# One core, decode attention over a 64k cache: heads in turn through one ring of 4 MB loads, in place of all keys first and all values after

## Chip, cores, metric

One core of one Trainium2 chip. The metric is the device time of one execution in microseconds (us). Times are medians of runs in the fast state, each measured beside runs of the kernel before on the same chip. A ratio is the mean time of one kernel's fast runs over that of the other's fast runs of the same rounds, so it is not quite the ratio of the medians that stand beside it.

## The reference, cut to what matters

```python
# x: 1 x 1 x 448; k_cache, v_cache: 1 x 8 heads x 65536 keys x 256, bf16
q = (layernorm(x) @ wq)                      # 16 query heads, two to each key head
scores = q . k * 256 ** -0.5                 # per head, over 65536 keys
o = softmax(scores) @ v
out = x + o @ wo + moe_branch(layernorm(x))  # the second branch has 4.8 MB of weights
```

Everything is bf16. The two caches are 537 of the 549 MB that are read, and each value is read once and used for two query heads.

## The kernel before

It works in two stages. The first reads the keys of all eight heads, four heads at a time. TensorE transposes each block of 128 keys by 128 positions, VectorE and ScalarE copy the result from PSUM (where this kernel has TensorE's results), TensorE multiplies by the query (QK) and joins the four heads' scores (JT in the code). Then one softmax is made for all heads. The second stage reads all values and multiplies them by the probabilities (P.V). Loads are 2 MB each, in six buffers, of which two lie over the query weights.

```python
JN_K = 16; HPC = 2; JV = 32; KV_NBUF = 6; NTB = 6; PV_COLGROUPS = 1
# ... loads, issued by SyncE in the order of use: all keys, then all values
for cc in range(total):
    buf = cc % KV_NBUF
    if cc >= KV_NBUF:
        wait("sp", "pe", ("KFREE", cc - KV_NBUF))
    # ... keys: 2 heads x 16 keys per partition; values: 32 keys per partition
    sp.dma_start(kvK[buf], src).then_inc(semK[buf], 16)
# ... transposes: 8 of 128 x 128 into one PSUM bank
for hf in range(NH):
    for jj in range(GNV):
        ins = pe.matmul(ps_t[tb][:, blk * P:(blk + 1) * P],
                        lhsT=kvK[buf][:, mm, nn0 + jj, hf * P:(hf + 1) * P],
                        rhs=ident_bf[:, :], is_transpose=True, start=True, stop=True)
# ... QK: four column groups of the array, one head in each
ins = pe.matmul(qb[po:po + rep, 0:512], lhsT=qT_sb[:, hf, h * rep:(h + 1) * rep],
                rhs=kt_buf[kt][:, hf * 512:(hf + 1) * 512],
                start=(hf == 0), stop=(hf == NH - 1), tile_position=(0, po))
# ... P.V: one accumulation for a head, two keys per matmul
ins = pe.matmul(ob[0:2 * rep, 0:2 * Dh], lhsT=lhsT, rhs=kvV[buf][:, j:j + 2, :],
                start=(n == 0), stop=(n + 2 >= NPP))
# ... the order on TensorE
for s in range(NSET):            # all keys
    # ... transposes of set s + 1, JT of set s - 1, QK of set s
pe_phase2a()                     # maximum over all scores, then the exponentials on ScalarE
for v in range(NCHV):            # all values
    pe_PV_chunk(v)
```

## Time and profile before

| | kernel before |
|---|---|
| time, median (range) | 1345.17 us (1344.43 to 1345.67) |
| profiled span | 1344.0 us |
| TensorE busy, granted clock | 85%, 0.986 |
| bytes moved, mean rate | 550.94 MB, 410 GB/s |
| rate with keys (200 to 700 us) | 407 GB/s |
| rate with values (740 to 1320 us) | 428 GB/s |

The prediction shows the lines behind this table. Two more are needed later. The first is from the page's table of DMA queues (packets, MB, share of the sixteen engines' span). The second is from the windows view (window; busy times of the engines; granted clock, DMA share, GB/s).

```profile
q8 instruction: 107, 1.75, 0.5%
1330.00:1336.00 6.00, 3.65 (x17) 1.31 (x18) 0.00 (x0) 0.00 (x0) 0.00 (x0) 1.00 0.35 147
```

The page labels queue 8 as instruction: it carries the program of an engine, in 107 pieces of 16 KB, the first at 27.5 us and the last at 1333.9 us, so while the kernel runs. It looks negligible. In the last six microseconds of loads the rate is 147 GB/s and the DMA share 0.35: the sixteen DMA engines do not finish together (the landings of the last load lie between 1330.9 and 1335.9 us).

### The profile page before, as it was taken

Reading aid. Unit: us, or ns where it says so; the run is one execution under the profiler, and the core shown is the slowest. Engines: PE = TensorE matmul, PEld = TensorE weight load, DVE = VectorE, ACT = ScalarE, POOL = GpSimd, SP = SyncE. Lnnn points to the kernel's source line nnn. Section 1 sums busy time; section 2 is a strip of 40 time slices with the busy share of each in tenths; the row PEclk is TensorE's granted clock in tenths of the full one; section 3 lists DMA queues with packets and bytes.
Section 4 is the critical chain, followed back from the end, with each engine's and each line's share of the span. In section 5 each row is a group of like instructions: output and inputs, shape, how many; then the busy total and the mean of one; then the engine's idle time right before and its main releaser. Section 6 shows DMA issues by size and latency. Waiting matters only on the chain.

```text
span 1344.0 us, 29602 instructions
## 1 busy us (share of the span) xinstructions
PE 1146.2 (85%) x13639; PEld 720.9 (54%) x13639; DVE 550.0 (41%) x859; ACT 429.6 (32%) x554; POOL 3.1 (0%) x19
## 2 busy tenths in 40 slices
PE   4979989999999999999996998777767777777776
PEld 4857867787777877777773443222222222222222
DVE  2767767777877878787773000000000000000000
ACT  1544645565555555555557600000000000000000
POOL 0000000000000000000000000000000000000000
PEclk9999999999999999999997899999999999999999
DMA  9999999999999999999997999999999999999996
GB/s 369 420 383 420 420 400 420 417 414 403 405 410 407 407 398 407 397 406 409 402 407 325 430 428 427 428 428 427 428 426 428 428 429 428 428 428 428 428 428 277
DMA packets 60738, 550.94 MB, mean 410 GB/s; under 512 B 4227, under 2 KB 10118, under 8 KB 11014
## 3 DMA queue, kind: packets, MB, share of 16 engines
q1 hardware_dynamic: 60610, 549.05, 98.5%
q8 instruction: 107, 1.75, 0.5%
q14 instruction: 17, 0.14, 0.0%
q10 hardware_dynamic: 4, 0.00, 0.0%
HBM read 549.03 MB, written 0.00 MB: 409 GB/s over the span
## 4 chain that ended last, share of the span: by engine, by line
PE 55%; DMA 40%; DVE 4%; ACT 1%; issue 0%; SPq 0%; DVEq 0%; ACTq 0%
DMA kv_buf<-in_A_v_cache_dram 34%; PE ps_t L359 33%; PE ps_t L513 10%; PE ps_q L384 9%; DMA kv_buf<-in_A_k_cache_dram 3%; DMA regA<-in_A_k_cache_dram 2%; DVE kt_buf L619 2%; PE ps_s L403 1%; DVE m1p L645 1%; PE ps_q L437 1%; DVE S_sb L641 1%; PE ps_t L453 1%; ACT S_sb L844 0%; ACT kt_buf L621 0%; PE ps_t L466 0%
## 5 line engine op out<-in xcount | busy, mean ns | idle before, releaser
L619 DVE COPY kt_buf<-ps_t 128x1024 bf16<-128x1024 bf16 x768 | 505.6, 688 | 170.6 <-PE ps_t L359 94.7
L513 PE MATMUL ps_t<-kv_buf,S_sb 128*4 128x512 bf16 x1376 | 313.4, 382 | 92.7 <-DMA kv_buf<-in_A_v_cache_dram 87.5
L359 PEld LDWEIGHTS ps_t<-ident_bf,kv_buf 128*128 128x128 bf16 x5504 | 313.2, 99 | 106.9 <-DVE kt_buf L619 70.2
L359 PE MATMUL ps_t<-ident_bf,kv_buf 128*128 128x128 bf16 x5504 | 341.8, 221 | 32.2 <-DMA kv_buf<-in_A_k_cache_dram 17.3
L621 ACT ACTIVATE kt_buf<-ps_t 128x1024 bf16<-128x1024 bf16 x256 | 262.0, 1023 | 299.5 <-PE ps_q L384 298.7
L513 PEld LDWEIGHTS ps_t<-kv_buf,S_sb 128*4 128x4 bf16 x1376 | 111.6, 85 | 290.6 <-DMA kv_buf<-in_A_v_cache_dram 121.6
L762 DVE CAST ob_sb<-ps_t 128x512 bf16<-128x512 f32 x8 | 5.5, 692 | 451.9 <-PE ps_t L513 451.9
L513 PE MATMUL ps_t<-regA,S_sb 128*4 128x512 bf16 x672 | 153.7, 383 | 43.1 <-DMA regA<-in_A_v_cache_dram 43.1
L359 PEld LDWEIGHTS ps_t<-ident_bf,regA 128*128 128x128 bf16 x2688 | 151.8, 98 | 48.8 <-DVE kt_buf L619 34.4
L359 PE MATMUL ps_t<-ident_bf,regA 128*128 128x128 bf16 x2688 | 165.7, 220 | 12.0 <-DVE kt_buf L619 7.4
L384 PE MATMUL ps_q<-kt_buf,qT_sb 128*2 128x512 bf16 x2048 | 154.9, 379 | 0.0
L513 PEld LDWEIGHTS ps_t<-regA,S_sb 128*4 128x4 bf16 x672 | 54.7, 85 | 139.8 <-DMA regA<-in_A_v_cache_dram 59.4
L629 ACT ACTIVATE s_1<-ps_q 98x512 bf16<-98x512 f32 x128 | 75.6, 591 | 0.9 <-PE ps_q L384 0.9
L629 ACT ACTIVATE s_0<-ps_q 98x512 bf16<-98x512 f32 x128 | 75.6, 591 | 0.0
L770 DVE TENSOR_TENSOR oT_sb<-ps_q,rs 128x4 bf16<-128x4 f32 x8 | 1.3, 162 | 95.3 <-PE ps_q L533 95.3
L844 ACT ACTIVATE S_sb<-S_sb,negmax 128x512 bf16<-128x512 bf16 x16 | 36.8, 2744 | 3.0 <-DVE negmax L715 3.0
L403 PE MATMUL ps_s<-sel_bf,s_0 128*128 128x8 bf16 x512 | 31.4, 167 | 1.7 <-ACT s_0 L629 1.7
L403 PE MATMUL ps_s<-sel_bf,s_1 128*128 128x8 bf16 x512 | 31.4, 167 | 0.8 <-ACT s_1 L629 0.7
L384 PEld LDWEIGHTS ps_q<-kt_buf,qT_sb 128*2 128x2 bf16 x2048 | 26.2, 79 | 5.7
L403 PEld LDWEIGHTS ps_s<-sel_bf,s_0 128*128 128x128 bf16 x512 | 26.4, 97 | 2.2 <-ACT s_0 L629 2.2
L403 PEld LDWEIGHTS ps_s<-sel_bf,s_1 128*128 128x128 bf16 x512 | 26.1, 97 | 1.7 <-ACT s_1 L629 1.7
L729 DVE TENSOR_TENSOR gs_sb<-ps_t,sg_sb 128x14 f32<-128x14 f32 x1 | 0.2, 173 | 45.0 <-ACT sg_sb L854 45.0
(70 smaller groups left out, 110.1 us busy)
## 6 DMA issues: line engine op xcount, KB each, us to landing
kv_buf<-in_A_k_cache_dram SPq DMA_DIRECT2D x86, 2048.0 KB, 14.4
kv_buf<-in_A_v_cache_dram SPq DMA_DIRECT2D x86, 2048.0 KB, 25.7
regA<-in_A_k_cache_dram SPq DMA_DIRECT2D x42, 2048.0 KB, 14.0
regA<-in_A_v_cache_dram SPq DMA_DIRECT2D x42, 2048.0 KB, 25.7
wo_sb<-in_A_wo_dram SPq DMA_DIRECT2D x1, 3584.0 KB, 21.8
regA<-in_A_wq_dram SPq DMA_DIRECT2D x1, 3072.0 KB, 10.3
regF<-in_B_w_down_dram SPq DMA_DIRECT2D x1, 1568.0 KB, 22.0
regF<-in_B_w_gate_dram SPq DMA_DIRECT2D x1, 1344.0 KB, 13.1
```

The source lines that it names most:

```text
L359: ins = pe.matmul(ps_t[tb][:, blk * P:(blk + 1) * P], lhsT=kvK[buf][:, mm, nn0 + jj, hf * P:(hf + 1) * P], rhs=ident_bf[:, :], is_transpos ...
L384: ins = pe.matmul(qb[po:po + rep, 0:512], lhsT=qT_sb[:, hf, h * rep:(h + 1) * rep], rhs=kt_buf[kt][:, hf * 512:(hf + 1) * 512], start=(hf ...
L403: ins = pe.matmul(ps_s[:, col:col + QW], lhsT=s2[s % 2][:, jj * P:(jj + 1) * P], rhs=sel_bf[:, :], start=True, stop=True)
L437: ins = pe.matmul(ps_p0[0:P, col:col + 1], lhsT=wq_sb[0:r, kc, q * Dh + hf * P:q * Dh + (hf + 1) * P], rhs=xnT_sb[0:r, kc:kc + 1], start=( ...
L453: ins = pe.matmul(ps_f[0:P, base + f:base + f + 1], lhsT=wsb[0:r, kc, f * P:(f + 1) * P], rhs=xnT_sb[0:r, kc:kc + 1], start=(kc == 0), sto ...
L513: ins = pe.matmul(ob[0:2 * rep, 0:2 * Dh], lhsT=lhsT, rhs=kvV[buf][:, j:j + 2, :], start=(n == 0), stop=(n + 2 >= NPP))
L619: ins = eng.tensor_copy(out=kt_buf[kt][:, :], in_=ps_t[tb][:, :])
L621: ins = eng.activation(out=kt_buf[kt][:, :], in_=ps_t[tb][:, :], func=ACTF.Copy)
L629: ins = act.activation(out=s2[s % 2][0:QROWS, :], in_=ps_q[0:QROWS, :], func=ACTF.Copy) if ctx.emit else None
L641: ins = dve.tensor_copy(out=S_sb[:, quad, n_lo:n_lo + SB_N, :], in_=ps_s[:, 0:W])
L645: ins = dve.tensor_reduce(out=m1p[:, quad, k, :], in_=S_sb[:, quad, n_lo:n_lo + SB_N, :].rearrange("p n q -> p q n"), axis=AX.X, op=ALU.max)
L844: ins = act.activation(out=ap, in_=ap, func=ACTF.Exp, bias=negmax[:, c:c + 1], scale=1.0, accum_out=rowsum[:, c:c + 1])
```

## The change

The intent is to keep the DMA engines at their rate from the start to the end. Heads are worked through one by one. Each head has its own softmax, and the key chunks of head h+1 alternate with the value chunks of head h. All loads, weights too, go through one ring in SBUF of 168 KB per partition, 4 MB a load (32 KB per partition). P.V accumulates in four column groups of the array, which are added when the result is transposed. The core of the diff, cut:

```diff
-JN_K = 16
-HPC = 2
-JV = 32
-KV_NBUF = 6
+RING = 86016                      # bf16 elements per partition: 5.25 loads of 64 x 256
+K_CHUNKS = [64] * 8
+V_LAST = [64] * 7 + [32, 16, 8, 8]
-PV_COLGROUPS = 1
 ...
+    for n, k_ in enumerate(ks):
+        kv_item(*k_)
+        if n >= len(K_FIRST) + 1:
+            v_next()              # one value chunk after each key chunk
+    while vs:
+        v_next()
 ...
+    def prog_sp():
+        for n, it in enumerate(items):
+            for m in range(max(0, it["need"] - 8), it["need"] + 1):
+                wait("sp", "pe", ("FREE", m))      # the loads whose space this one takes
 ...
-                ins = pe.matmul(ob[0:2 * rep, 0:2 * Dh],
-                                lhsT=lhsT, rhs=kvV[buf][:, j:j + 2, :],
-                                start=(n == 0), stop=(n + 2 >= NPP))
+                ins = nc.tensor.matmul(ps_o[32 * g:32 * g + 2 * rep, :], lhsT=S[:, k:k + 2, :].rearrange("p n i -> p (n i)"), rhs=kv[:, j:j + 2, :],
+                                       start=(k < 2 * NG), stop=(k >= NPP - 2 * NG), tile_position=(0, 32 * g))
 ...
+            post("dve", lambda: dve_scopy(h, k))
+            if k == NSB - 1:
+                post("dve", lambda: dve_m1(h))
+                defer(2, lambda: pe_m1t(h), ("sm", h))   # the head's softmax, some sets later
```

## The prediction

> **What bounds the kernel now.** I read the forty slices first, because the shares of section 1 (PE 85%, DVE 41%) average over two stages with different limits. Page of the kernel before, sections 2 and 3:
>
> ```profile
> PE   4979989999999999999996998777767777777776
> DVE  2767767777877878787773000000000000000000
> DMA  9999999999999999999997999999999999999996
> GB/s 369 420 383 420 420 400 420 417 414 403 405 410 407 407 398 407 397 406 409 402 407 325 430 428 427 428 428 427 428 426 428 428 429 428 428 428 428 428 428 277
> q1 hardware_dynamic: 60610, 549.05, 98.5%
> ```
>
> One slice is 33.6 us. Slices 0 to 20 are the keys, 22 to 39 the values. The values run flat at 428 GB/s, the keys at about 405, with a hole (325) between. The DMA digit is 9 in both stages, so it does not tell a full queue from one that is merely never empty; the GB/s row does.
>
> What sets the rate in each stage, from the windows (columns: window, PE, PEld, DVE, ACT, POOL busy, granted clock, DMA share, GB/s) and the list of waits (who waited for whom: total us, times, longest):
>
> ```profile
> 200.00:700.00 500.00, 482.08 (x8429) 394.15 (x8426) 398.87 (x611) 289.51 (x384) 0.00 (x0) 1.00 1.00 407
> 740.00:1320.00 580.00, 454.45 (x2116) 167.93 (x2113) 7.50 (x20) 19.65 (x18) 0.00 (x0) 0.99 1.01 428
> SPq L299 <- PE ps_t L359: 562.1, 64, 20.1
> PEld ps_t L359 <- DMA kv_buf<-in_A_k_cache_dram: 17.9, 2, 9.0
> PE ps_t L513 <- DMA kv_buf<-in_A_v_cache_dram: 87.5, 71, 2.8
> ```
>
> In the key stage PE is busy 482 of 500 us and waits for a key load only twice; the load queue waits for PE's transposes instead (562 us). The chain of waits shows the pace there: sets of 1.05 MB start every 2.51 us (1.89 transposes, 0.08 join, 0.53 QK), and every 16 sets one is 4.0 us because the score copy (0.69) and the maximum (1.1) sit ahead of VectorE's PSUM copies. That is 16 x 2.51 + 1.5 = 41.7 us for 16.8 MB, 402 GB/s: PE with its evacuation is the bound. In the value stage PE waits for every chunk: DMA is the bound. The seam and the end, in the chain:
>
> ```profile
> 721.40 4.84 ACT S_sb L844 x4
> 726.34 33.32 PE ps_t L513 x144
> 1310.29 25.63 DMA kv_buf<-in_A_v_cache_dram
> 1335.97 3.63 PE ps_t L513 x16
> ```
>
> The softmax over all heads stands between the stages with all buffers full of values: the windows 725 to 730 and 730 to 735 moved 52 and 134 GB/s.
>
> [...] QK, which already uses four column groups:
>
> ```profile
> L384 PE MATMUL ps_q<-kt_buf,qT_sb 128*2 128x512 bf16 x2048 | 154.9, 379 | 0.0
> L513 PE MATMUL ps_t<-kv_buf,S_sb 128*4 128x512 bf16 x1376 | 313.4, 382 | 92.7 <-DMA kv_buf<-in_A_v_cache_dram 87.5
> ```
>
> The same 512 columns cost 154.9/2048 = 76 ns each there, against 313.4/1376 = 228 ns in P.V. [...] after 8.4 us of waiting at 92 us the window 100 to 105 has clock 0.50 and 32 transposes took 3.60 us, not 1.96.
>
> **The change, part by part.** All four parts serve one aim: never let DMA fall below its rate.
>
> 1. Interleaving. After head 0, key and value chunks of 4.19 MB alternate. A pair takes 8.39 MB / 428 = 19.6 us of DMA. PE per pair: keys 4 sets, 10.05 us, plus a quarter of the 1.5 us stall, 10.4; values 32 matmuls x 76 ns = 2.4. Together 12.9 us warm. PE will then idle some 6.7 us per pair and fall to half clock; from the cold example a first set costs about 4.6 instead of 2.5, so I add 2.6: 15.5 us, still 4 below DMA. PE leaves the path. Gain: the key stage from 110 to 700 us ran at 408 instead of 428, 590 x (1 - 408/428) = 27.6 us, of which about 1 us stays for the output weights; plus about 1 us before 110.
>
> 2. Softmax per head. Head h's maximum and two exponentials (2 x 2.74 us) run while the loads of other heads stream. Gain: the seam, 5 x (1 - 52/428) + 5 x (1 - 134/428) = 7.8 us. Its new cost, some 10 us of stall in a PE that has 4 to 6.7 us of slack per pair, is absorbed by the ring.
>
> 3. Ring. From the sizes in the code, 13 to 17 MB of later loads lie between most loads and the one whose space they take (10 to 13 MB around the FFN weights and each output-weight piece): 23 to 40 us of DMA. PE's lag must stay below that. Its worst is head 0, keys alone: PE at 10.4 us per 4.19 MB against 9.8 of DMA, starting about 10 us late because of the 128 query matmuls (9.06 us). After 40 sets, ten chunks' worth, the lag is 10 + 10 x 0.6 = 16 us, below 39. I expect no blocking.
>
> 4. P.V in four groups: 467 us of PE busy (313.4 + 153.7) become about 155. Hidden as such, but part 1 would fail without it: 32 x 228 ns = 7.3 us of values plus 10.4 + 2.6 is 20.3, above 19.6. The last chunk shrinks from 16 matmuls (3.63 us) to 4: 3.2 us off the end.
>
> What stays: the start and small rows of weights (slices 0 to 3 lose about 9 us, of which I keep 8), the end after the values (ob copy to output 4.4 us) and the skew of the engines before it (from 1330 to 1335 the rate falls 295, 213, 180, 164, 33).
>
> Sum from above: 26.6 + 1 + 7.8 + 3.2 = 38.6 off 1345, 1306. Sum from below: all transfers, 550.94 MB / 428 = 1287; start and small rows 8.6; skew 3.8; last matmuls, rest and the gap between span and time 0.4 + 4.4 + 1.0. Total 1305. Loads grow from 8 or 16 KB to 32 KB per partition: key windows with a full queue (424 to 430 for 8 KB) hardly differ from value windows (428 for 16 KB), so I allow 0.2%, 3 us, and predict **1303 us**.
>
> **Rivals.** (a) **PE stays the bound.** For: its clock will drop, and ScalarE's exponentials block its share of the PSUM copies 5.5 us per head, with one PSUM buffer per position now (four, not six). Against: 4 us of slack per pair even cold, and a PE that falls behind is busy and warm. If the pair took 22 us, 55 pairs would add 130 us: slower than before. I give this 3%. (b) **The ring blocks** in head 0 or at the FFN weights, where only 10 MB (23 us) are ahead: a few stalls of 5 to 10 us, 1310 to 1325. For: lag 16 us there at its worst plus ffn1's 112 matmuls (7.6 us before). Against: by then five pairs have won back 4 us each. 10%. (c) **The rate of 32 KB rows.** Nothing in this trace has rows as long. At 432 GB/s the time falls to about 1293; if two alternating streams cost 1% it is 1316. (d) **The time is hidden anyway**: that the keys at 405 are DMA's own limit with 8 KB rows, and stay. Against: windows of 428 with key loads while PE waits (95 to 100 us), and PE waiting for keys only twice.
>
> **Range and chances.** The floor of 428 and the ends are measured; what spreads is the rate (plus or minus 0.7%, 9 us) and small ring stalls. Range 1292 to 1314. 2% faster means below about 1318.5: 0.91. Within 2%: 0.07, from (b) or (c) at their bad ends. Slower: 0.02, from (a).
>
> **What would show it.** Right: GB/s about 428 in nearly all slices from the third on, no hole; the chain mostly of DMA; PE waiting for the ring's loads in every pair; P.V matmuls at some 75 to 80 ns of busy time each; PE share about 65 to 70% with granted clock clearly below 1, at no cost; the queue's waits for PE long in total but never emptying DMA. Wrong: slices around 400 with PE at 9 (rival a), single low slices near 100 or 200 us (b), or a flat rate other than 428 (c).

## The result, and the profile after

The changed kernel takes **1310.41 us** (1310.06 to 1310.87, 4 runs) against 1345.17. The ratio is 0.9738, with a 95% interval of 0.9724 to 0.9752: faster by 2.6%. That is inside the stated range, 7 us above the stated time.

Page of the changed kernel, slices (32.7 us each) and queues:

```profile
PE   5998765867866767667767668667677577676444
PEclk9999878878879888788788788788788887888666
DMA  9999999999999999999999999999999999999995
GB/s 383 426 427 429 415 382 432 430 430 431 431 430 425 432 428 430 431 428 431 430 430 427 429 429 430 430 430 430 428 428 429 428 426 433 429 429 416 434 426 213
q1 hardware_dynamic: 24578, 549.04, 98.4%
q8 instruction: 107, 1.75, 0.5%
```

The rate is flat from slice 6 to slice 38 (mean 429.1), and the hole between the stages is gone. TensorE falls to some 7 tenths, and its granted clock to 8. Apart from the start (slice 0, 383), the low slices are 4 and 5 (415, 382), with the small rows of the second branch's weights (a row of 896 bytes took 41 ns, 21.9 bytes per ns, one of 3584 bytes 151 ns, 23.7; a row of 32 KB took 1215 ns, 27.0), 36 (416, a loss of 1 us), and the last with 213.

Windows of the changed kernel (columns as before), in the steady part and at the end of the loads:

```profile
250.00:1280.00 1030.00, 714.31 (x10482) 541.22 (x10479) 409.55 (x669) 324.18 (x421) 0.00 (x0) 0.83 1.00 429
1288.00:1303.40 15.40, 7.15 (x64) 1.58 (x64) 0.00 (x0) 0.00 (x0) 0.00 (x0) 0.57 0.42 177
```

For 1030 us the engines move 429 GB/s; then for 15 us they are 42% busy. Before, this ragged end had 6 us. From the list of waits of the changed kernel (total us, times, longest), TensorE's wait for keys and the load queue's wait for TensorE:

```profile
PE ps_t L370 <- DMA ring<-in_A_k_cache_dram: 308.0, 55, 10.4
SPq L298 <- PE ps_s L431: 870.1, 61, 19.6
```

TensorE now waits for nearly every key chunk. The queue waits for TensorE too, 870 us in all, but its loads are issued some 40 us before they land (44.3 us for keys, 37.9 for values), so DMA does not run dry. The groups (count, then busy us and mean ns):

```profile
L370 PE MATMUL ps_t<-ident_bf,ring 128*128 128x128 bf16 x8192 | 598.1, 241 | 309.8 <-DMA ring<-in_A_k_cache_dram 308.0
L658 PE MATMUL ps_o<-ring,S_sb 128*4 128x512 bf16 x2048 | 136.6, 412 | 48.1 <-DMA ring<-in_A_v_cache_dram 46.1
L398 PE MATMUL ps_q<-kt_buf,qT_sb 128*2 128x512 bf16 x2048 | 167.9, 407 | 0.0
```

P.V fell from 467 us of busy time to 136.6. Over 2048 matmuls that is 67 ns each: the 412 ns of the line are the time of one from start to end, and several overlap. The last instructions, in order of time (start, duration):

```profile
1303.33 0.60 PE L658 MATMUL ps_o<-ring,S_sb 128*4 128x512 bf16 x4 [0.64 <-DMA ring<-in_A_v_cache_dram]
1303.98 0.69 DVE L511 CAST ob_sb<-ps_o 100x512 bf16<-100x512 f32 x1 [61.95 <-PE ps_o L658]
1304.73 0.27 PE L531 MATMUL ps_m<-sel_bf,ob_sb 100*128 100x2 bf16 x4 [0.80 <-DVE ob_sb L511]
1305.24 1.65 PE L557 MATMUL ps_m<-ring,oT_sb 128*1 128x448 bf16 x4 [0.25 <-DVE oT_sb L518]
1306.93 0.61 DVE L543 TENSOR_TENSOR res_bf<-ps_m,rowsf 1x448 bf16<-1x448 f32 x1 [1.74 <-PE ps_m L557]
```

From the last landing to the end of the span it is 5.8 us. From 1303.4 to 1309 us the granted clock is 0.50, and the output product takes 1.65 us.

**Where the predicted sum and the result part.** From the slices: 550.89 MB at 429.1 GB/s are 1284 us; slices 0 to 5 lose 8.5 us against that rate; slice 39 loses 16.5. Together 1309, the span. The prediction had 1284 (1287 less 3 for longer rows), 8.6, and for the end 3.8 + 0.4 + 4.4 = 8.6, and 1 us between span and time. So one term was wrong: the end. Of the 16.5 us, 5.8 follow the last landing. The other 10.7 are the ragged end, which the prediction calls skew and put at 3.8.

**A first look at the ragged end.** The trace records sixteen landings for each load, and for 97% of the span fifteen to seventeen data packets are in flight; each landing is read here as that of one of the sixteen DMA engines. Sorted, for loads along the changed kernel's run (us; this table is worked out from those records):

```
load complete   1st engine    8th      9th     16th    pieces of program so far
      83.2         81.4       82.3     82.9     83.2        8
     247.2        243.0      243.9    246.6    247.2       24
     447.0        439.7      441.4    446.3    447.0       ~40
     647.0        635.1      637.8    644.8    647.0       ~57
     845.6        830.5      834.2    843.3    845.6       ~73
    1044.1       1025.9     1030.5   1041.8   1044.1       ~90
    1303.3       1285.2     1287.7   1301.0   1303.3      107
```

The sixteen engines part into two groups of eight. At the end the first group has finished about 1286 us, the other about 1302. The distance between the groups' means, set against the number of pieces fetched on queue 8, is a straight line through zero: 1.31 us for each piece per engine of a group of eight, correlation 0.994. Against time the line is as straight (0.993), so this alone does not tell pieces from bytes. Single pieces do show in the records: between the loads complete at 547.2 and 606.7 us five pieces were fetched, and five landings of the late group moved back against the early group, each by about 1.4 us, while its other three stayed. The packet of a piece itself took 1.07 us (median), a data row of the same 16 KB 0.62. In the kernel before the same 107 pieces give no such line (correlation 0.08): the groups were 3.9 us apart at 282 us but only 1.3 at 650 us, after 80 pieces, and in its value stage, with 17 pieces, the distance grew from 0.5 to 3.4.

This suggests **theory F**: each 16 KB piece of TensorE's program that is fetched holds one of eight DMA engines back by 1.31 us. While TensorE sets the pace the late engines catch up; when DMA sets it they fall behind for good, and the late group ends the kernel. Its **rival R** is that eight engines are slower by nature, so that the distance grows with bytes.

### The profile page after: what moved, and what is told of

It reads as the page before. It is cut to its first block, busy times and chain, and to the rows that moved or that the text cites.

```text
span 1309.1 us, 29128 instructions
## 1 busy us (share of the span) xinstructions
PE 921.8 (70%) x13690; PEld 701.4 (54%) x13690; DVE 537.7 (41%) x885; ACT 426.6 (33%) x555; POOL 4.5 (0%) x34
## 2 busy tenths in 40 slices
DMA packets 24701, 550.89 MB, mean 421 GB/s; under 512 B 2371, under 2 KB 6214, under 8 KB 7366
## 3 DMA queue, kind: packets, MB, share of 16 engines
q8 instruction: 107, 1.75, 0.5%
## 4 chain that ended last, share of the span: by engine, by line
DMA 75%; PE 25%; SPq 0%; issue 0%; DVE 0%
DMA ring<-in_A_k_cache_dram 68%; PE ps_t L370 17%; DMA ring<-in_A_v_cache_dram 7%; PE ps_q L398 4%; PE ps_o L658 2%; PE ps_s L431 1%; PE ps_m L557 0%; SPq L298 0%; PE ps_m L608 0%; PE ps_m L531 0%; DVE ob_sb L511 0%; DVE res_bf L543 0%; PE ps_m L502 0%; DVE oT_sb L518 0%
## 5 line engine op out<-in xcount | busy, mean ns | idle before, releaser
L370 PE MATMUL ps_t<-ident_bf,ring 128*128 128x128 bf16 x8192 | 598.1, 241 | 309.8 <-DMA ring<-in_A_k_cache_dram 308.0
L370 PEld LDWEIGHTS ps_t<-ident_bf,ring 128*128 128x128 bf16 x8192 | 552.0, 110 | 423.8 <-DMA ring<-in_A_k_cache_dram 336.1
L352 DVE COPY kt_buf<-ps_t 128x1024 bf16<-128x1024 bf16 x768 | 493.2, 686 | 636.9 <-PE ps_t L370 636.2
L383 ACT ACTIVATE s<-ps_q 98x512 bf16<-98x512 f32 x256 | 152.9, 597 | 335.5 <-PE ps_q L398 335.5
L658 PE MATMUL ps_o<-ring,S_sb 128*4 128x512 bf16 x2048 | 136.6, 412 | 48.1 <-DMA ring<-in_A_v_cache_dram 46.1
L398 PE MATMUL ps_q<-kt_buf,qT_sb 128*2 128x512 bf16 x2048 | 167.9, 407 | 0.0
L658 PEld LDWEIGHTS ps_o<-ring,S_sb 128*4 128x4 bf16 x2048 | 49.3, 89 | 122.1 <-DMA ring<-in_A_v_cache_dram 54.3
L431 PE MATMUL ps_s<-sel_bf,s 128*128 128x8 bf16 x1024 | 64.9, 169 | 0.7 <-ACT s L383 0.7
L431 PEld LDWEIGHTS ps_s<-sel_bf,s 128*128 128x128 bf16 x1024 | 57.2, 102 | 2.4 <-ACT s L383 1.6
L477 ACT ACTIVATE S_sb<-S_sb,negmax 128x512 bf16<-128x512 bf16 x16 | 13.4, 861 | 7.3 <-DVE negmax L470 7.2
## 6 DMA issues: line engine op xcount, KB each, us to landing
ring<-in_A_k_cache_dram SPq DMA_DIRECT2D x63, 4096.0 KB, 44.3
ring<-in_A_v_cache_dram SPq DMA_DIRECT2D x63, 4096.0 KB, 37.9
ring<-in_A_wo_dram SPq DMA_DIRECT2D x8, 448.0 KB, 30.3
ring<-in_A_wq_dram SPq DMA_DIRECT2D x1, 3072.0 KB, 10.4
ring<-in_A_k_cache_dram SPq DMA_DIRECT2D x2, 1024.0 KB, 15.1
```

Of the source, the lines that this page charges most:

```text
L352: op(e, ("EV", g), lambda x: x.tensor_copy(out=kt[:, :], in_=tb[:, :]))
L370: ins = nc.tensor.matmul(ps_t[g % NTB][:, blk * P:(blk + 1) * P], lhsT=kv[:, j + GN * m + jj, hf * P:(hf + 1) * P], rhs=ident_bf[:, :], is ...
L383: op("act", ("EVQ", s), lambda e: e.activation(out=s2[s % 2][0:QROWS, :], in_=ps_q[0:QROWS, :], func=ACTF.Copy))
L398: ins = nc.tensor.matmul(ps_q[32 * m:32 * m + rep, 0:512], lhsT=qT_sb[:, hf, h * rep:(h + 1) * rep], rhs=kt[:, hf * 512:(hf + 1) * 512], s ...
L431: ins = nc.tensor.matmul(o, lhsT=s2[s % 2][:, jj * P:(jj + 1) * P], rhs=sel_bf[:, :, :], start=True, stop=True)
L477: op("act", ("EXPI", h, i), lambda e, i=i: e.activation(out=S[:, :, i], in_=S[:, :, i], func=ACTF.Exp, bias=negmax[:, h, i:i + 1], scale=1 ...
```

## The experiments

All eleven ran without an error. Each is given with its median, its ratio to the kernel before in the same rounds, and the difference to the changed kernel's ratio (0.9738) times 1345 us, because the kernel before differed by up to 2 us between batches. A ratio's interval is about plus or minus 0.0014, or 2 us. The changed kernel was not run again in these batches, so a difference of two ratios is uncertain by about 2.7 us (an estimate from the two intervals).

| run | median us | ratio | against the changed kernel |
|---|---|---|---|
| a_halfT: half of the transposes | 1304.97 | 0.9690 | -6.5 us |
| a_vsplit: P.V matmuls in two | 1314.09 | 0.9758 | +2.7 us |
| a_poolfetch: longer idle program | 1332.09 | 0.9891 | +20.6 us |
| a_low8: one load on few engines | 1341.46 | 0.9963 | +30.3 us |
| a_pv1: P.V in one group | 1312.82 | 0.9747 | +1.2 us |
| a_seq: no interleaving | 1311.23 | 0.9737 | -0.1 us |
| a_ring3: ring of 3.25 loads | 1327.01 | 0.9856 | +15.9 us |
| b_pv4: kernel before, P.V in four | 1340.70 | 0.9957 | -5.8 us to before |
| a_wolow8: output weights on few engines | 1338.05 | 0.9944 | +27.7 us |
| a_wolow8half: every other head so | 1325.50 | 0.9850 | +15.1 us |
| a_f32T: transposes of 4-byte pairs | 1305.51 | 0.9699 | -5.2 us |

### Fewer instructions, the same loads: a_halfT

```diff
-        for hf in range(NH):
+        for hf in range(1):
             for jj in range(GN):
                 blk = hf * GN + jj
```

The PSUM banks are zeroed once, so that nothing unwritten is read. The scores lack half their positions; the output still passed the comparison, presumably because the scores here are so small that the softmax is nearly uniform.

> The changed kernel with the second half of all key transposes left out (4096 matmuls and 4096 weight loads fewer; wrong result on purpose; the instruction memory of TensorE shrinks from 107 to 75 pieces of 16 KB). Theory F: each piece of program that is fetched holds back one of eight DMA engines by 1.31 us, and these eight set the end. Then 32 pieces fewer bring the last landing 32/8 x 1.31 = 5.2 us forward: about 1305 us, and the gap between the two groups of eight engines at the end falls from 16.2 to about 11 us. Rival R (eight engines are slower by nature, so the gap grows with bytes): 1310 us and a gap of 16 us, because TensorE is off the path either way.

Measured: 1304.97 us. The queue table of this run:

```profile
q8 instruction: 75, 1.23, 0.4%
```

The pieces fell from 107 to 75. That is 32 pieces for the 8192 TensorE instructions left out, 256 instructions a piece, so queue 8 carries TensorE's program. The late group ended at 1296.0 us instead of 1301.8, 5.8 earlier (expected 5.2). The distance at the end is 13.2 us, not 11: the early group too came in earlier, by 2.9 us, which F does not say; the two groups seem tied to some degree. Rival R, which allowed no change, falls: no byte of data was taken away. That TensorE became faster is no explanation by itself, for it is off the path (a_pv1 below slows it a good deal for 1.2 us).

### More instructions, the same work: a_vsplit

```diff
-                ins = nc.tensor.matmul(ps_o[32 * g:32 * g + 2 * rep, :], ..., rhs=kv[:, j:j + 2, :], ...)
+                for n2 in range(2):
+                    ins = nc.tensor.matmul(ps_o[32 * g:32 * g + 2 * rep, n2 * Dh:(n2 + 1) * Dh], ..., rhs=kv[:, j + n2, :], ...)
```

> The changed kernel with every P.V matmul of 512 columns split into two of 256 (right result, the same columns; 2048 matmuls and 2048 weight loads more, 16 pieces of program more). Theory F: 16/8 x 1.31 = 2.6 us later, 1313 us, gap 18.8 us. Rival R: 1310 us, gap 16 us.

Measured: 1314.09 us, +2.7 us by the ratios. The queue table of this run:

```profile
q8 instruction: 123, 2.02, 0.6%
```

There are 123 pieces. The late group ended 3.3 us later (1305.1). The distance is 17.0 us, not 18.8: again the early group moved with it. By time alone this run is at the edge of the uncertainty; with the landings it agrees with F in sign and size.

### A longer program on an idle engine: a_poolfetch

```diff
+            for _ in range(16384):
+                nc.gpsimd.wait_ge(sem_prog["pool"], 1)     # long satisfied
```

> The changed kernel with 16384 waits already satisfied added to the otherwise idle GpSimd program (0.5 MB, about 32 pieces of 16 KB; touches no data). Theory F, if GpSimd's program comes over the same eight engines: 5.2 us later, 1315.6 us, gap 21 us. If it comes over the other eight: the time stays at 1310 us and the gap shrinks to about 11 us. Rival R: nothing changes, 1310 us and 16 us.

Measured: 1332.09 us. Page of this run, rates and the queue of the added program:

```profile
GB/s 374 427 430 426 411 341 411 435 424 430 431 429 424 430 424 427 431 420 419 369 429 428 429 428 373 428 432 408 433 429 427 432 428 428 428 432 425 432 431 186
q14 instruction: 76, 0.62, 0.1%
```

The expectation failed in size: +20.6, not +5.2. The landings show why. GpSimd's program came on queue 14, in 64 more pieces of 8 KB (76 for 12, 0.62 MB for 0.10), and all held back one engine. For a load complete at 643.5 us fifteen engines had landed by 620.0, and the sixteenth 23.5 us later. The program waits for all sixteen landings of a load (in the changed kernel the last load's sixteenth is at 1303.3 us, and its first matmul starts at 1303.33), so the ring waits for that one engine: the slices with 341, 369 and 373. That was the most: the added pieces were nearly all fetched by 730 us, and at the end the one engine was still 9.4 us behind the next. Half a megabyte of a program that does nothing cost 20 us, and by the landings all of it came over one engine. This confirms the core of F (program fetch delays particular DMA engines, and the latest engine ends the kernel) and refutes its detail that there are always eight.

### Moving data from the late engines to the early: a_low8, a_wolow8, a_wolow8half

If the late group could carry less data, both would end about 1294 us (an estimate: halfway between 1286 and 1302). So in a_low8 one 4 MB value load was cut into sixteen loads of 8 partitions, four apart, and in the other two runs the output-weight loads in the same way. In the trace each small load has eight landings, after one record at its issue, where a load of 128 partitions has sixteen. Which eight engines these are no trace shows; that they are the early ones was the assumption in the two runs with output weights.

```diff
+        for base in range(0, P, 32):
+            for i in range(4):
+                def d(a, r=slice(base + i, base + 32, 4)):
+                    ...
+                ds.append(d)
```

> The changed kernel with one 4 MB value load cut into 16 loads of 8 partitions each, which should run on eight DMA engines only (4.2 MB on one group instead of 2.1 on each). If these are the eight that are ahead, the late group is relieved of 2.1 MB, 9.7 us: the last landing comes 6 to 8 us earlier, about 1303 us[...]. If these are the eight that are late, the end moves 9.7 us out, about 1320 us.

> The changed kernel with the eight output-weight loads (3.67 MB in all) cut into loads of 8 partitions[...] (right result). Theory F: the late group is relieved of 64 rows of 1792 B per engine per two heads, 8 x 16 x 74 ns = 9.5 us in all, the early group takes 9.5 us more: both end about 1294 to 1296 us after the start instead of 1286 and 1302; time 1302 to 1305 us, gap at the end under 4 us. If the small loads hold up the engines, as the value load cut in the same way did: 1310 to 1320 us.

> The same for every other head only: half the relief, 4.7 us, so 1305 to 1307 us and a gap of about 7 us. If the gain is not from the balance of the engines, no such proportion.

Measured: 1341.46, 1338.05 and 1325.50 us, all slower than without, and outside all that was expected. The rates of a_low8, where the cut load is in slices 22 to 24:

```profile
GB/s 374 433 424 432 405 399 432 429 428 434 423 434 428 428 431 430 427 432 424 434 428 432 372 220 399 431 429 396 428 429 433 426 407 434 427 432 425 434 425 152
```

Its pieces landed from 754 to 808 us, a stretch longer than the ring's 39 us of loads, and the last of them came in pairs, 1.8 us apart, so two engines were much later than the rest. In a_wolow8 fourteen engines did end within 3.1 us of each other, at 1319 to 1322 us, but the other two landed at 1331, 12 us behind the mean of the fourteen. Full and half dose cost 27.7 and 15.1 us, roughly in proportion. So these small loads do not take eight engines at an even pace, and cost more than they move (the full dose is 3.67 MB, 8.6 us at 429 GB/s). Whether a better balance would win the 7 us stays open. What made two engines so late was not found.

### P.V in one column group again: a_pv1

```diff
-            g = (k // 2) % NG
+            g = 0
 ...                           # start and stop follow
```

> The changed kernel with P.V in one column group (one part undone). The prediction's sentence: a pair of chunks takes TensorE 20.3 us against 19.6 of DMA, so TensorE becomes the bound, and 55 pairs at 0.7 us more give about 1349 us. My theory now: TensorE would then idle only 1.9 us per pair, stay warm, and need 17.7 us; DMA stays the bound, 1310 to 1312 us with the granted clock near 1.

Measured: 1312.82 us, +1.2 us, which is within the uncertainty. Page of this run, clock and P.V group:

```profile
PEclk9999979999999999899999899999999999999899
L658 PE MATMUL ps_o<-ring,S_sb 128*4 128x512 bf16 x2048 | 457.6, 382 | 18.4 <-DMA ring<-in_A_v_cache_dram 16.4
```

TensorE does 321 us more work and the time hardly moves: it has that much slack, and its clock stays up (0.962 for 0.836 in the changed kernel), with waits for keys of 103.1 us in all and 5.3 at the longest (308.0 and 10.4 there). The prediction's sentence that the interleaving would fail without the four groups is refuted.

### No interleaving: a_seq

```diff
-    for n, k_ in enumerate(ks):
-        kv_item(*k_)
-        if n >= len(K_FIRST) + 1:
-            v_next()
+    for h in range(Hkv):
+        for k_ in [k for k in ks if k[2] == h]:
+            kv_item(*k_)
+        while vs and vs[0][2] == h:
+            v_next()
 ...                           # a head's softmax is finished before its first values
```

> The changed kernel without interleaving: all key chunks of a head, then all its value chunks, through the same ring. If the interleaving itself is needed (softmax of a head has nothing to hide behind), about 10 us per head stay open, 1390 us. My theory: TensorE falls behind by 8 x 0.6 us in the keys and by 10 us in the softmax, 15 us in all, less than the 39 us of loads in the ring, and catches up in the values: 1310 us plus or minus 3.

Measured: 1311.23 us, the same. Page of this run, TensorE and rate:

```profile
PE   5995438984399734996359954599436994389844
GB/s 379 425 428 391 404 429 427 427 429 432 429 430 429 429 430 431 428 428 428 430 431 428 428 430 429 429 427 429 432 430 428 429 428 431 429 430 428 429 430 206
```

TensorE swings between 9 tenths in a head's keys and 3 in its values; the rate does not feel it. The ring carries TensorE across a head's keys and softmax. So chunk by chunk is not needed: it is enough that keys and values alternate head by head, and that the ring reaches that far. How much the deep ring would give in the old order, all keys first, no run tested. As an estimate from the prediction's figures (10.4 us of TensorE against 9.8 of DMA per key chunk), TensorE would fall 64 x 0.6 = 38 us behind in the keys, besides its late start (10) and the softmax (7.8), against a ring of 39 us: part of the gain might come from the ring alone.

### A shallower ring: a_ring3

```diff
-RING = 86016
+RING = 53248
```

> The changed kernel with a ring of 3.25 instead of 5.25 loads of 4 MB. Theory F (the late engines' own work sets the end; the deep ring only lets the others run ahead): not faster; 1310 to 1325 us, and the gap between the engine groups at the end at most 10 us. Rival (the depth lets the groups drift apart, and the drift costs the time): up to 8 us faster, 1302 to 1306 us.

Measured: 1327.01 us, 2 us above the range I gave. The rates of this run:

```profile
GB/s 379 427 429 428 413 357 324 433 427 401 435 429 429 424 398 434 427 428 397 429 431 430 428 399 426 436 428 424 394 432 432 429 428 400 429 432 425 431 431 312
```

The groups of engines are 2.5 us apart at the end: a shallow ring keeps them together. Yet it is slower, by stalls in slices 5 and 6 (the second branch's weights, called FFN weights in the prediction, where by the code only 4 to 6 MB of other loads lie between a load and the one whose space it takes) and one of about 2 us in each head (401, 398, 397, 399, 394, 400). The last slice does move more (312 for 213), so the end is less ragged, but the stalls cost more than that. The run mixes the two effects; what it shows is that keeping the groups together with a shallow ring did not pay.

### The kernel before with P.V in four groups alone: b_pv4

```diff
-                ins = pe.matmul(ob[0:2 * rep, 0:2 * Dh], ...)
+                g = (n // 2) % PV_COLGROUPS
+                ins = pe.matmul(ob[32 * g:32 * g + 2 * rep, 0:2 * Dh], ..., tile_position=(0, 32 * g))
 ...                           # a selector matrix adds the groups when the result is transposed
```

> The kernel before with P.V in four column groups alone. In its value stage DMA is the bound, so only the seam after the softmax (buffers free sooner, about 2.5 us) and the last chunk (about 2 us) can gain: 1340 to 1343 us, the same within 2%.

Measured: 1340.70 us, ratio 0.9957. Windows of this run at the seam (the softmax between the stages) and in the values:

```profile
725.00:730.00 5.00, 3.50 (x36) 1.23 (x40) 0.00 (x0) 5.00 (x5) 0.00 (x0) 0.50 0.38 131
730.00:735.00 5.00, 3.80 (x68) 1.34 (x60) 0.00 (x0) 5.00 (x5) 0.00 (x0) 0.95 0.98 393
740.00:1320.00 580.00, 238.73 (x2072) 58.15 (x2072) 7.50 (x20) 19.94 (x20) 0.00 (x0) 0.52 1.01 428
```

The value stage keeps its 428 GB/s at a granted clock of 0.52. The seam moves 131 and 393 GB/s instead of 52 and 134, 5 x (79 + 259) / 428 = 3.9 us, and after the last landing 1.0 us is saved (7.1 instead of 8.1). This part is worth 5 to 6 us in the old order; in the new order (a_pv1) the 1.2 us are within the uncertainty.

### A version that is faster than both: a_f32T

Two neighbouring bf16 positions of a key are transposed as one 4-byte value. One transpose then serves 128 keys by 256 positions, and even and odd positions lie side by side; the query is split to match.

```diff
-        kv = ap_of(n).rearrange("p (j d) -> p j d", d=Dh)
-        for hf in range(NH):
-            for jj in range(GN):
-                blk = hf * GN + jj
-                ... lhsT=kv[:, j + GN * m + jj, hf * P:(hf + 1) * P], rhs=ident_bf[:, :], is_transpose=True
+        kv = ap_of(n).bitcast(FP32).rearrange("p (j d) -> p j d", d=P)
+        for jj in range(GN):
+                ... lhsT=kv[:, j + GN * m + jj, :], rhs=ident_f[:, :], is_transpose=True
 ...
-                                           rhs=kt[:, hf * 512:(hf + 1) * 512],
+                                           rhs=kt[:, hf:1024:2],
 ...
-                               lhsT=w[0:r, kc, q * Dh + hf * P:q * Dh + (hf + 1) * P],
+                               lhsT=w[0:r, kc, q * Dh + hf:(q + 1) * Dh:2],
```

> The changed kernel with each pair of neighbouring bf16 key values transposed as one 4-byte value: one transpose per 128 keys instead of two, the query split into even and odd positions to match (right result if the transpose passes the bits through). TensorE's program shrinks from 107 to 75 pieces, as in the run with half the transposes left out, so theory F gives about 1305 us and a gap of about 13 us, if TensorE stays off the path. Rival: the 4-byte weight loads, 256 ns each in the traces against 106, make a set cost 16 x 256 + 700 = 4.8 us and a pair of chunks 21.6 us against 19.6 of DMA: TensorE is the bound again, about 1400 to 1460 us.

Measured: **1305.51 us** (1304.75 to 1305.58), ratio 0.9699 (0.9685 to 0.9712), 5.2 us under the changed kernel, with the right result. Page of this run, queue 8 and the transposes:

```profile
q8 instruction: 75, 1.23, 0.4%
L369 PE MATMUL ps_t<-ident_f,ring 128*128 128x128 f32 x4096 | 603.0, 310 | 297.6 <-DMA ring<-in_A_k_cache_dram 295.7
L369 PEld LDWEIGHTS ps_t<-ident_f,ring 128*128 128x128 f32 x4096 | 537.0, 161 | 414.2 <-DMA ring<-in_A_k_cache_dram 323.7
```

Half as many transposes take the same busy time (603.0 against 598.1 us), so TensorE is no faster. The loads are the same, TensorE's work is the same; only its program is shorter, by 32 pieces. F gives 5.2 us for that; 5.2 us were measured (2.5 to 7.9 with the uncertainty), and the late group ends at 1296.8 instead of 1301.8. With a_halfT, where the work did fall, this is the clearest case for F. Its figure of 1.31 us is rough, though: with the same 107 pieces the groups ended 16.2 us apart in the changed kernel, 17.3 in a_pv1 and 19.1 in a_seq. The rival, 4.8 us a set because of slow 4-byte weight loads, is refuted: 16 transposes take 1.97 us at a granted clock of 1.00 (40 to 110 us), as long as 32 of 2-byte data in the kernel before (1.96).

## Why the prediction was right, point by point

- **What bounds the kernel before** was right. With keys and values mixed the rate is 429 over 33 slices, and the key chunks run at it too. That alone does not refute rival d, since the key rows also grew from 8 to 32 KB; what speaks against it is the window of 95 to 100 us before, where key loads with 8 KB rows ran at 428 while TensorE waited. (A small slip: TensorE waited for key loads three times, not twice; the third, 5 us, is listed under regA.)
- **Part 1, interleaving.** The gain of about 28 us is in the trace: no slice near 405 between 6 and 38. But the reason given was too narrow. a_seq has the gain without the interleaving of chunks. What carries it, as far as the runs go, is that each head's keys are followed by values within the ring's reach, so that TensorE's mean load counts; the share of the ring alone was not tested. The clock did fall (0.83 from 250 to 1280 us), the first set of a chunk cost 3.6 us of transposes instead of 1.96 (at 247.3 us, after a wait of 6.1 us; in the kernel before 3.3 and 3.6 after 4.6 and 8.4 us), and it cost nothing, as said.
- **Part 2, softmax per head.** Right: the seam is gone, and the softmax of the heads is not seen in the rate.
- **Part 3, ring.** Right that it does not block in head 0 or at the FFN weights, where slices 4 and 5 lose 4.7 us to small rows but DMA stays busy (a share of 1.01 from 144 to 190 us). a_ring3 shows that it would at 3.25 loads (rival b in a smaller ring).
- **Part 4, P.V in four groups.** The busy time was right (136.6 us against about 155). The claim that part 1 would fail without it was wrong (a_pv1, +1.2 us): 2.6 us for a cold clock were added, where in a_pv1 the granted clock stayed at 0.962.
- **The rate of 32 KB rows** (rival c): 429.1, 0.26% above 428 where 0.2% was allowed. Nothing in the trace before had such rows, so this allowance was a guess that came true. Whether the engines can give more no run shows.
- **The sum.** The one badly mis-sized term is "skew 3.8", taken over from the kernel before: measured 10.7. The total stayed in the range although part 4's claim was wrong, because the sum is built on DMA's rate and TensorE's time does not enter it. The rest of the end was 1.0 us longer (5.8 for 4.4 + 0.4), partly by the output product at clock 0.50 (1.65 us for 0.92). The step that failed is to carry the skew over as if it were fixed. In the kernel before most of the program (90 of 107 pieces) was fetched by the end of the key stage, where TensorE set the pace; the change moved the bound to DMA for the whole span, and so made the program's 1.75 MB, spread unevenly, part of the path: 107/8 x 1.31 = 17.5 us on the late engines, by F (measured distance at the end: 16.2). That those catch up where TensorE sets the pace is read from the landings of the kernel before; no run tested it apart.

## What to carry to other kernels

When a change makes DMA the bound everywhere, ask what else uses the DMA engines and whether it is spread over all sixteen: here the latest engine ended each load and the kernel (the two groups were 16.2 us apart at the end), and the mean rate of 429 GB/s did not show it. The unrolled program was itself traffic (1.75 MB on queue 8; 64 bytes an instruction on TensorE, from 256 to a piece of 16 KB), so in this kernel fewer, larger instructions were worth more (a_f32T, 5.2 us) than faster ones (a_pv1, 1.2 us for 321 us of TensorE work). For hiding a stage, mixing work of both kinds within the reach of a deep ring was enough; the finer order and the faster matmuls that seemed necessary were not needed.
